# Normalising attention after the product with V: inverted sums broadcast through DRAM

## The chip, the cores and the metric

The kernel runs on one core of a Trainium2 chip. The metric is the device time of one execution in microseconds, the median of several runs. The core has TensorE (matrix products; the profile calls it PE and its weight loads PEld), VectorE (DVE), ScalarE (ACT) and GpSimd (POOL), and DMA engines that move data between DRAM and the on-chip memory. DMAs are started from the instruction queues of SyncE (SP) and ScalarE. TensorE writes only into PSUM, whose banks have to be emptied by VectorE or ScalarE before they can be used again. Each engine works its own queue strictly in order; an instruction that waits holds all behind it.

## The reference

Eight batches with eight heads each, 576 positions, head size 64. Attention is causal by blocks of 64 positions, and its output feeds a gated layer:

```python
scores = (1 / sqrt(D)) * q @ k.T            # per batch and head
scores = where(block_i >= block_j, scores, -1e9)
scores = scores - max(scores, axis=-1)
attn = exp(scores)
attn = attn / (sum(attn, axis=-1) + 1e-9)
x = (attn @ v)                              # heads side by side: 4608 x 512
out = (sigmoid(x @ w_gate) * (x @ w_val)) @ w_out   # d_ff = 1536
```

Everything is 32-bit. The division by the row sum can stand before the product with v or behind it: each row of the output is scaled by one number either way.

## The kernel before

**Attention** goes by pairs of heads, 32 pairs in all: a pair fills the 128 partitions with 2 x 64. For each pair K and Q are brought into transposed form (`prep`), and `attend` does the rest. The queries lie in blocks of 128 rows, i = 0 to 3, and a tail of 64 rows for each of the two heads (block 4, both heads in one tile, `Pt`). Block i sees 128 (i + 1) keys. `s_blocks` and `s_tail` form the scores in PSUM (L356), overwrite what is masked (L387, L389), take the negative row maximum (L367, L403, VectorE), and take the exponential on ScalarE (L370, L405), which leaves P in SBUF and, with `accum_out`, the row sums in columns of `sm`. Since `sm` has the queries on its partitions, a row's sum is a number per partition for P.

`recip` adds 1e-9 to columns of `sm` and inverts them (L409, L410, VectorE), twice a pair. `norm` multiplies the four P tiles by them per head (L419 on VectorE; in pairs 4 to 7 block 3 goes to ScalarE, L417), and `norm_t` the tail (L480 on VectorE, L478 on ScalarE). Then TensorE transposes P in pieces of 128x128 (`tr_main`, `tr_low`, `tr_tail`, L245), ScalarE copies the transposed pieces to `G1` and `G0` (`copy_out`, L345), and `av` multiplies: V is the stationary operand, G the moving one, and the result is x^T, head dimension on the partitions and queries along the row, in two pieces of 320 and 256 columns. ScalarE copies it from PSUM to `xT` (L345, called from L463); `finish` makes from it the rounded part `XH` (L470), the rest `XL` (L473, GpSimd), and stores `xT` to DRAM (L471).

**The gated layer** has 12 blocks of d_ff. Four are done in the same pass (`mlp1`, L126 and L135), batch by batch, their matmuls dealt out one by one between those of attention. The other eight follow after attention in a second pass (L838, L896), which reads x back from DRAM. Both take weights that are first converted from how they lie in the inputs (`convert`, L106 to L118; `sums_gv`, `split_gv` and others, L631 to L699), mostly on VectorE. The glue `h` (L147) empties PSUM on VectorE.

**Order.** A pair has a slot of 12 ticks. `FIRST` (pairs 0 to 6), `TURN` (pair 7) and `REST` (from pair 8) list the steps of a slot with the ticks behind each: a name in small letters is a step of this pair p; `AV` and the ones with `TR` in capitals belong to pair p - 1. So A V of a pair runs in the slot of the next one. In each tick some matmuls of `mlp1` are dealt out. Weight conversion, loads of q, k and v (two and three pairs ahead, on SyncE's queue) and, at the end, the early work for the second pass hang on these ticks. A planner orders each engine's instructions by a simulated timeline; it keeps to data dependencies, buffers that have to come free, and to explicit orders: `behind(a, b)` puts instruction a after b on its engine. `mark(engine, ins)` notes the last attention instruction of an engine in `last`, and other work is put behind it: the conversions (L78 and L106, L108), K's and Q's transposes (L276), and the early work:

```python
            if when == (0, TICKS - 2):
                sums_gv(*early[0], alone=last["DVE"])
            if when == (1, 1):
                x_sums(early_x[0], nc.vector, last["DVE"])
            if when == (1, 4):
                sums_gv(*early[1], alone=last["DVE"])
```

Here (0, t) is tick t of the last pair's slot and (1, t) is tick t of one more slot, in which only A V of the last pair is left; its ticks come after A V.

PSUM has three double banks for attention (scores, transposes and A V take them in turn) and two single banks for `mlp1`.

Of the kernel before, what the change touches and what calls it, by code (L numbers as in the profile page):

```python
# [20 lines left out]
N2 = 384  # L21
# [9 lines left out]
         ("tr3", 1))  # L31
REST = (("s", 3), ("t", 1), ("AV", 2), ("tr3", 1), ("k", 0), ("tr2", 1), ("q", 0), ("trl", 2), ("trt", 2))
TURN = (("s3", 1), ("TR2", 1), ("k", 0), ("s2", 1), ("TRt", 1), ("q", 0), ("t", 1), ("TRl", 1), ("sl", 1), ("AV", 1),
        ("tr3", 1), ("tr2", 1), ("trl", 1), ("trt", 1))
# [6 lines left out]
def attn_glu_kernel(ctx: ExitStack, tc: tile.TileContext, q, k, v, w_gate, w_val, w_out, out):  # L41
# [119 lines left out]
    with ExitStack() as s2:  # L161
# [29 lines left out]
        for QB in QBs + [x.bitcast(F32) for x in QBS]:  # L191
            nc.gpsimd.memset(QB, 0.0)
        wg, wv = {}, {}
# [137 lines left out]
        def attend(p):  # L331
# [6 lines left out]
            sm = at.tile([P, 12], F32, name="sm", bufs=2)  # L338
            keep = {}
            col = {3: 0, 2: 2, 4: 4, 1: 5, 0: 7}  # L340
            rest = p > N_FIRST
            by_act = NP <= p <= N_FIRST
# [20 lines left out]
            def softmax(ps, i, c):  # L363
                n = P * (i + 1)
                c0 = col[i]
                Pi = keep[i] = p_tile(i)
                mark("DVE", nc.vector.tensor_reduce(out=nm[:, c0:c0 + 2], in_=ps[:, :, c:c + n], axis=AX.X, op=ALU.max,  # L367
                                                    negate=True))
                for h in range(2):
                    mark("ACT", nc.scalar.activation(out=Pi[:, h], in_=ps[:, h, c:c + n], func=AF.Exp,  # L370
                                                     bias=nm[:, c0 + h:c0 + h + 1], accum_out=sm[:, c0 + h:c0 + h + 1]))
# [21 lines left out]
            def s_tail():  # L393
# [4 lines left out]
                for half in range(2):  # L398
                    for k, (x, y) in enumerate(ops):
# [6 lines left out]
                                                 func=AF.Exp, bias=nm[:, c0:c0 + 1], accum_out=sm[:, c0:c0 + 1]))  # L406

            def recip(a, n):
                nc.vector.tensor_scalar_add(sm[:, a:a + n], sm[:, a:a + n], 1e-9)  # L409
                nc.vector.reciprocal(sm[:, a:a + n], sm[:, a:a + n])  # L410

            def norm(i):
                c0 = col[i]
                Pi = keep[i]
                for h in range(2):
                    if i == 3 and by_act:
                        mark("ACT", nc.scalar.mul(out=Pi[:, h], in_=Pi[:, h], mul=sm[:, c0 + h:c0 + h + 1]))  # L417
                        continue
                    mark("DVE", nc.vector.tensor_scalar_mul(Pi[:, h], Pi[:, h], sm[:, c0 + h:c0 + h + 1]))  # L419
# [55 lines left out]
            def norm_t():  # L475
                r = sm[:, col[4]:col[4] + 1]
                if by_act:
                    nc.scalar.mul(out=keep[4], in_=keep[4], mul=r)  # L478
                else:
                    nc.vector.tensor_scalar_mul(keep[4], keep[4], r)  # L480

            def first_step(what):
                if what[0] == "s":
                    if what == "sl":
                        norm(3)
                    s_blocks({"s3": (3,), "s2": (2,), "sl": (1, 0)}[what])
                elif what == "t":
                    s_tail()
                    recip(0, 5)
                elif what == "tr3":  # L490
                    norm(2)
                    norm_t()
                    tr_main(3)
                elif what == "tr2":
                    recip(5, 4)
                    norm(1)
                    norm(0)
                    tr_main(2)
                else:
                    step(what)  # L500

            def step(what):
                if what == "s":
                    s_blocks((3,), (2,), (1, 0))
                    recip(0, 4)
                    norm(3)
                elif what == "t":
                    s_tail()
                    norm(2)
                    recip(4, 5)  # L510
                elif what == "tr3":
                    tr_main(3)
                    norm(1)
                    norm(0)
                    norm_t()
# [10 lines left out]
            return step if rest else first_step  # L526
# [13 lines left out]
        def tiles_o(i):  # L540
            if not co_:
                co_.append(at.tile([P, 5, 512], U32, name="co", bufs=1))
            co, j = co_[0], 2 * (i % 2)
            return (co[:, j:j + 2].rearrange("p a (n w) -> p (a n) w", w=2), co[:, 4], None,
# [484 lines left out]
```

## Time and profile before

| | |
|---|---|
| runs, median (lowest to highest) | 1223.63 us (1222.17 to 1224.56) |
| the profiled execution: its span, first to last instruction | 1223.3 us |
| TensorE busy | 1171.9 us, 96% |
| VectorE busy | 861.9 us, 70% |
| ScalarE busy | 651.2 us, 53% |
| GpSimd busy | 337.9 us, 28% |
| attention and the first pass | to about 656 us |
| second pass | from about 656 us |

The profile is of one execution, whose own time is known by its span alone. Times are in microseconds from its start; in groups of instructions `out<-in` names the tiles, and after the bar come the busy time, the mean in ns of one instruction, and the idle time of the engine just ahead of the group, with what ended it. "A <- B" in the lists of waits says that A waited until B was done.

### The profile page before, as it was taken

What the parts mean: (1) busy time and instruction counts of PE and PEld (TensorE: products, weight loads), DVE (VectorE), ACT (ScalarE), POOL (GpSimd) and SP (SyncE); (2) the same over time, 40 slices, a digit from 0 to 9 for tenths busy, and PEclk for the clock granted to TensorE, in tenths of its full rate; (3) what the DMA queues carried; (4) which work ended last, traced back from release to release, by engine and by line L of the source; (5) the groups of instructions that cost most, each with busy time, mean ns of one, the idle gap of its engine ahead of it and who ended that gap; (6) DMA issues with size and microseconds to landing.
All of it is one profiled execution on the core that took longest, in us unless ns stands there. A gap on an engine that the chain in (4) does not pass through costs nothing.

```text
span 1223.3 us, 20662 instructions
## 1 busy us (share of the span) xinstructions
PE 1171.9 (96%) x7421; PEld 1030.8 (84%) x7421; DVE 861.9 (70%) x1691; ACT 651.2 (53%) x1523; POOL 337.9 (28%) x409
## 2 busy tenths in 40 slices
PE   6889899999999999999999999999999999999996
PEld 4567678888888888889798899999999998998995
DVE  6888876577575875757898967857866755755742
ACT  5778766666665776756544544444444322422420
POOL 1113232223222332313401132132132152361441
PEclk8889999999999999999999999999999999999998
DMA  8543242423424333332343245145197154264243
GB/s 212 130 103 90 53 109 43 113 68 63 109 60 102 70 76 85 76 86 82 97 147 128 62 160 190 41 166 187 37 326 289 55 180 140 77 197 136 79 148 103
DMA packets 239125, 142.91 MB, mean 117 GB/s; under 512 B 183600, under 2 KB 204080, under 8 KB 238384
## 3 DMA queue, kind: packets, MB, share of 16 engines
q1 hardware_dynamic: 227968, 122.43, 35.7%
q10 hardware_dynamic: 11056, 19.17, 4.4%
q8 instruction: 59, 0.97, 0.3%
q14 instruction: 42, 0.34, 0.1%
HBM read 94.37 MB, written 47.19 MB: 116 GB/s over the span
## 4 chain that ended last, share of the span: by engine, by line
PE 74%; DVE 14%; DMA 4%; ACT 4%; issue 2%; SPq 1%; POOL 1%; POOLq 0%; DVEq 0%; ACTq 0%
PE b L838 23%; PE bank L242 11%; PE m L126 11%; PE m L896 9%; PE m L135 7%; PE b L896 5%; PE bank L245 4%; DMA pr<-part_d 2%; DVE P L419 2%; ACT P L370 2%; DVE XL L730 2%; PE bank L126 1%; DVE nm L367 1%; PE bank L135 1%; DVE KQ L274 1%
## 5 line engine op out<-in xcount | busy, mean ns | idle before, releaser
L838 PE MATMUL b<-XH,w 128*128 128x384 f32 x1344 | 349.9, 336 | 5.4 <-DVE v L874 2.7
L838 PEld LDWEIGHTS b<-XH,w 128*128 128x128 f32 x1344 | 243.7, 188 | 12.6 <-DVE v L874 6.6
L838 PE MATMUL b<-XL,w 128*128 128x384 f32 x672 | 223.7, 335 | 0.0
L370 ACT ACTIVATE P<-bank,nm 128x512 f32<-128x512 f32 (+3 forms) x256 | 132.9, 533 | 86.4 <-DVE nm L367 74.7
L838 PEld LDWEIGHTS b<-XL,w 128*128 128x128 f32 x672 | 126.1, 188 | 1.2
L896 PE MATMUL m<-wo,hH 128*128 128x512 f32 x384 | 124.9, 391 | 0.0
L345 ACT COPY G<-bank 128x768 f32<-128x768 f32 (+3 forms) x160 | 106.2, 700 | 27.4 <-PE bank L245 26.0
L367 DVE TENSOR_REDUCE nm<-bank 128x2 f32<-128x1024 f32 (+3 forms) x128 | 104.8, 819 | 8.2 <-ACT P L370 5.7
L126 PE MATMUL m<-XH,wv 128*128 128x288 f32 x448 | 104.8, 304 | 2.9 <-DVE h L147 2.9
L126 PE MATMUL m<-XH,wg 128*128 128x288 f32 x448 | 106.1, 305 | 0.6 <-ACT t L145 0.6
L153 POOL TENSOR_TENSOR hL<-h,hH 128x288 fp32r<-128x288 f32 (+1 forms) x56 | 49.0, 875 | 182.4 <-ACT hH L152 171.7
L242 PE MATMUL bank<-G,VS 128*64 128x320 f32 (+4 forms) x896 | 95.2, 364 | 0.0
L245 PE MATMUL bank<-ident,P 128*128 128x128 f32 x640 | 90.0, 280 | 4.1 <-DVE P L419 3.6
L911 POOL TENSOR_TENSOR pr<-pr,pr 128x512 f32<-128x512 f32 x36 | 48.2, 1342 | 162.7 <-DMA pr<-part_d 117.0
L419 DVE TENSOR_SCALAR P<-P,sm 128x256 f32<-128x256 f32 (+3 forms) x248 | 87.8, 414 | 1.7
L242 PEld LDWEIGHTS bank<-G,VS 128*64 128x64 f32 x896 | 56.4, 138 | 36.8 <-issue 4.1
L245 PEld LDWEIGHTS bank<-ident,P 128*128 128x128 f32 x640 | 76.7, 144 | 12.4 <-ACT wo L117 3.1
L861 ACT ACTIVATE g<-g 128x384 f32<-128x384 f32 x72 | 37.2, 524 | 87.2 <-DVE g L874 62.2
L896 PEld LDWEIGHTS m<-wo,hH 128*128 128x128 f32 x384 | 71.9, 188 | 13.8
L729 ACT CAST XH<-XB 128x1536 fp32r<-128x1536 f32 (+2 forms) x72 | 65.9, 939 | 29.3 <-DVE XB L727 22.5
L473 POOL TENSOR_TENSOR XL<-xT,XH 128x576 fp32r<-128x576 f32 x32 | 47.2, 1476 | 123.5 <-ACT XH L470 107.8
L126 PEld LDWEIGHTS m<-XH,wv 128*128 128x128 f32 x448 | 74.8, 188 | 6.2 <-DVE h L147 4.2
(176 smaller groups left out, 2543.6 us busy)
## 6 DMA issues: line engine op xcount, KB each, us to landing
pr<-part_d SPq DMA_DIRECT2D x72, 256.0 KB, 3.7
xT_d<-xT ACTq DMA_DIRECT2D x32, 288.0 KB, 2.8
XB<-xT_d SPq DMA_DIRECT2D x16, 576.0 KB, 5.5
part_d<-ost SPq DMA_DIRECT2D x36, 256.0 KB, 4.0
out_dram<-ost SPq DMA_DIRECT2D x36, 256.0 KB, 2.8
VS<-in_v_dram SPq DMA_DIRECT2D x64, 128.0 KB, 2.5
part_d<-ost ACTq DMA_DIRECT2D x32, 256.0 KB, 2.1
rqk<-in_k_dram SPq DMA_DIRECT2D x108, 72.0 KB, 2.6
```

Of the source, the lines that this page charges most:

```text
L126: mm = nc.tensor.matmul(ps, lhsT=lh, rhs=rh, start=(i == 0), stop=(i == n - 1))
L135: mm = nc.tensor.matmul(ps, lhsT=lh[:, f, t * P:(t + 1) * P], rhs=rh, start=(i == 0), stop=(i == n - 1))
L153: lower.tensor_sub(out=hL, in0=h2[:, cols], in1=hH.bitcast(F32))
L242: pe_last[:] = [nc.tensor.matmul(*args, **kw).ins]
L245: pe_last[:] = [nc.tensor.transpose(*args).ins]
L345: mark("ACT", nc.scalar.copy(out=dst, in_=src))
L367: mark("DVE", nc.vector.tensor_reduce(out=nm[:, c0:c0 + 2], in_=ps[:, :, c:c + n], axis=AX.X, op=ALU.max, negate=True))
L370: mark("ACT", nc.scalar.activation(out=Pi[:, h], in_=ps[:, h, c:c + n], func=AF.Exp, bias=nm[:, c0 + h:c0 + h + 1], accum_out=sm[:, c0 + h ...
L419: mark("DVE", nc.vector.tensor_scalar_mul(Pi[:, h], Pi[:, h], sm[:, c0 + h:c0 + h + 1]))
L729: nc.scalar.copy(out=XO[j][0][:, a:b], in_=x)
L838: mm = nc.tensor.matmul(ps, lhsT=lh, rhs=rh, start=(first and k == 0), stop=(k == n - 1), skip_group_check=not first)
L896: mm = nc.tensor.matmul(po[t], lhsT=lh[:, f, t * P:(t + 1) * P], rhs=rh, start=(half == 0 and i == 0), stop=(half == 1 and i == 5))
```

## The change

P is left undivided: `norm` and `norm_t` are gone, and so is the split of steps between `first_step` and `step`. The sums go to columns 4h + i (column 8 for the tail) of two fixed tiles of 128x32 that take turns. A new step `r`, without ticks of its own, stands in each list right after `tr3` of the same pair; it adds and inverts all nine columns at once, transposes the tile in blocks of 32x32 on VectorE, writes the nine rows to DRAM in four DMAs, and reads them back in four DMAs, each row sent to the 64 partitions of its head, so that the tile `rb` has the inverse of a query's sum in the query's column on every partition. `av` then takes x^T out of PSUM with a multiplication by `rb` on VectorE, where ScalarE had copied it; the multiplication is marked as VectorE's last, and so is the transpose.

To make room, the raw w_out pieces of the first pass are converted in two tiles that are used for x later on, and not in a tile of their own.

```diff
-        ("tr3", 1))
+        ("tr3", 1), ("r", 0))
...
-            sm = at.tile([P, 12], F32, name="sm", bufs=2)
+            sm = SMs[p % 2]
+            rb = at.tile([P, S], F32, name="rb", bufs=2)
...
-            def norm(i):
-                c0 = col[i]
-                Pi = keep[i]
-                for h in range(2):
-                    if i == 3 and by_act:
-                        mark("ACT", nc.scalar.mul(out=Pi[:, h], in_=Pi[:, h], mul=sm[:, c0 + h:c0 + h + 1]))
-                        continue
-                    mark("DVE", nc.vector.tensor_scalar_mul(Pi[:, h], Pi[:, h], sm[:, c0 + h:c0 + h + 1]))
+            def recip():
+                nc.vector.tensor_scalar_add(sm[:, :9], sm[:, :9], 1e-9)
+                nc.vector.reciprocal(sm[:, :9], sm[:, :9])
+                rT = at.tile([P, 32], F32, name="rT", bufs=2)
+                mark("DVE", nc.vector.transpose(out=rT, in_=sm))
+                r_d = dram.tile([9, P], F32, name="r_d", bufs=2)
+                for j in range(4):
+                    nc.sync.dma_start(out=r_d[:, 32 * j:32 * j + 32], in_=rT[32 * j:32 * j + 9])
+                for o, n, src in ((0, 4 * P, r_d[:8].rearrange("(h i) q -> h (i q)", h=2)),
+                                  (4 * P, D, r_d[8].rearrange("(h q) -> h q", h=2))):
+                    for h in range(2):
+                        nc.sync.dma_start(out=rb[rows(h), o:o + n], in_=src[h].partition_broadcast(D))
...
-                    copy_out(xT[:, q0:q0 + n], pv[:, i, :n])
+                    mark("DVE", nc.vector.tensor_mul(out=xT[:, q0:q0 + n], in0=pv[:, i, :n], in1=rb[:, q0:q0 + n]))
...
-            def norm_t():
-                r = sm[:, col[4]:col[4] + 1]
-                if by_act:
-                    nc.scalar.mul(out=keep[4], in_=keep[4], mul=r)
-                else:
-                    nc.vector.tensor_scalar_mul(keep[4], keep[4], r)
...
-                co_.append(at.tile([P, 5, 512], U32, name="co", bufs=1))
+                co_.extend(cv.tile([P, 6, N2], U32, name="XB", bufs=2) for _ in range(2))
```

More of the change, by code (lines that the diff above doesn't have):

```diff
@@ L30 @@
 FIRST = (("s3", 1), ("TR2", 1), ("k", 1), ("s2", 1), ("TRt", 1), ("q", 1), ("t", 1), ("TRl", 1), ("sl", 1), ("AV", 2),
-         ("tr3", 1))
-REST = (("s", 3), ("t", 1), ("AV", 2), ("tr3", 1), ("k", 0), ("tr2", 1), ("q", 0), ("trl", 2), ("trt", 2))
+         ("tr3", 1), ("r", 0))
+REST = (("s", 3), ("t", 1), ("AV", 2), ("tr3", 1), ("r", 0), ("k", 0), ("tr2", 1), ("q", 0), ("trl", 2), ("trt", 2))
 TURN = (("s3", 1), ("TR2", 1), ("k", 0), ("s2", 1), ("TRt", 1), ("q", 0), ("t", 1), ("TRl", 1), ("sl", 1), ("AV", 1),
-        ("tr3", 1), ("tr2", 1), ("trl", 1), ("trt", 1))
+        ("tr3", 1), ("r", 0), ("tr2", 1), ("trl", 1), ("trt", 1))
 N_FIRST = 7
@@ L192, in attn_glu_kernel @@
             nc.gpsimd.memset(QB, 0.0)
+        SMs = [at.tile([P, 32], F32, name=f"sm{i}") for i in range(2)]
+        for SM in SMs:
+            nc.gpsimd.memset(SM, 0.0)
         wg, wv = {}, {}
@@ L337, in attend @@
             nm = at.tile([P, 12], F32, name="nm", bufs=2)
-            sm = at.tile([P, 12], F32, name="sm", bufs=2)
+            sm = SMs[p % 2]
+            rb = at.tile([P, S], F32, name="rb", bufs=2)
             keep = {}
-            col = {3: 0, 2: 2, 4: 4, 1: 5, 0: 7}
+            col = {i: 2 * i for i in range(5)}
             rest = p > N_FIRST
-            by_act = NP <= p <= N_FIRST
             def copy_out(dst, src):
@@ L370, in softmax @@
                     mark("ACT", nc.scalar.activation(out=Pi[:, h], in_=ps[:, h, c:c + n], func=AF.Exp,
-                                                     bias=nm[:, c0 + h:c0 + h + 1], accum_out=sm[:, c0 + h:c0 + h + 1]))
+                                                     bias=nm[:, c0 + h:c0 + h + 1], accum_out=sm[:, 4 * h + i:4 * h + i + 1]))
             def s_blocks(*groups):
@@ L473, in finish, with step @@
                 nc.gpsimd.tensor_sub(out=XL[:, hp], in0=xT, in1=XH[:, hp].bitcast(F32))
-            def norm_t():
-                r = sm[:, col[4]:col[4] + 1]
-                if by_act:
-                    nc.scalar.mul(out=keep[4], in_=keep[4], mul=r)
-                else:
[L480 to L485, printed above, removed]
+            def step(what):
+                if what == "s":
+                    s_blocks((3,), (2,), (1, 0))
+                elif what[0] == "s":
                     s_blocks({"s3": (3,), "s2": (2,), "sl": (1, 0)}[what])
@@ L488, in first_step @@
                     s_tail()
[L489 to L510, printed above, removed]
+                elif what == "r":
+                    recip()
                 elif what == "tr3":
                     tr_main(3)
-                    norm(1)
-                    norm(0)
-                    norm_t()
                 elif what == "tr2":
@@ L524, in step @@
                     finish()
-            return step if rest else first_step
+            return step
         W_out = []
@@ L541, in tiles_o @@
             if not co_:
-                co_.append(at.tile([P, 5, 512], U32, name="co", bufs=1))
-            co, j = co_[0], 2 * (i % 2)
-            return (co[:, j:j + 2].rearrange("p a (n w) -> p (a n) w", w=2), co[:, 4], None,
+                co_.extend(cv.tile([P, 6, N2], U32, name="XB", bufs=2) for _ in range(2))
+            co = [x.rearrange("p a n -> p (a n)") for x in co_]
+            j = 1024 * (i % 2)
+            return (co[0][:, j:j + 1024].rearrange("p (n w) -> p n w", w=2), co[1][:, :512], None,
                     mp.tile([P, 512], F32, name="csq", tag="ost", bufs=2))
```

5 lines of the change are left out of this document (1 added, 4 removed).

## The prediction

> **What bounds the kernel now.** I read the page first, then the busy time by stretch, TensorE's waits, the chain of waits, the groups by shape and the timelines at both ends of the attention.
>
> ```profile
> span 1223.3 us, 20662 instructions
> PE 1171.9 (96%) x7421; PEld 1030.8 (84%) x7421; DVE 861.9 (70%) x1691; ACT 651.2 (53%) x1523; POOL 337.9 (28%) x409
> ```
>
> TensorE is busy for 1171.9 of 1223.3 us, and the change gives it neither more nor less to do. So a gain can only come out of its 51.4 us of idle time and out of stretches with a lower granted clock. Where these lie:
>
> ```profile
> 25.00:92.00 67.00, 56.16 (x365) 38.62 (x366) 56.16 (x124) 51.70 (x139) 12.09 (x14) 0.90 0.54 126
> 92.00:176.00 84.00, 76.95 (x543) 60.36 (x544) 68.32 (x146) 63.24 (x166) 24.47 (x32) 0.98 0.33 79
> 176.00:560.00 384.00, 382.41 (x2966) 332.35 (x2963) 259.60 (x552) 259.50 (x699) 114.24 (x188) 1.00 0.36 80
> 560.00:597.00 37.00, 33.95 (x278) 29.76 (x274) 31.11 (x67) 23.77 (x67) 10.13 (x16) 0.99 0.28 88
> 597.00:656.00 59.00, 56.95 (x339) 49.26 (x338) 53.90 (x118) 24.10 (x48) 8.62 (x4) 0.98 0.41 133
> 656.00:700.00 44.00, 41.63 (x226) 39.53 (x225) 42.76 (x75) 23.33 (x41) 6.03 (x4) 1.00 0.23 74
> ```
>
> After the stretch come TensorE, its weight loads, VectorE, ScalarE, GpSimd, then the granted clock. From 176 to 560 us, pairs 9 to 30, TensorE waits 1.6 us of 384: there the change can win nothing. From 25 to 176 us, pairs 0 to 8, it waits 10.8 + 7.1 = 17.9 us, and the clock of 0.90 and 0.98 costs 56.2 x 0.10 + 77.0 x 0.02 = 7.1 us more. From 597 to 700 us VectorE is busy for 96.7 of 103 us: work put there has hardly a gap to go to.
>
> ```profile
> PE bank L242 <- ACT P L370: 8.4, 4, 3.8
> ```
>
> And from the chain of waits (start, length, what), the first and the last of 18 pieces:
>
> ```profile
> 33.06 1.45 DVE P L419 x4
> ...
> 156.87 0.43 DVE Pt L480
> ```
>
> The first line is TensorE's largest wait between 10 and 92 us (sum, times, longest): for ScalarE's exponentials, which wait for row maxima, which stand in VectorE's queue among divisions. The 18 pieces are the divisions of P (L419 and L480, and L417 on ScalarE); they make 15.7 us of the chain.
>
>
> **The change part by part.** Durations from the groups by shape (busy time, mean ns):
>
> ```profile
> L419 DVE TENSOR_SCALAR P<-P,sm 128x256 f32<-128x256 f32 (+3 forms) x248 | 87.8, 414 | 1.7
> L480 DVE TENSOR_SCALAR Pt<-Pt,sm 128x576 f32<-128x576 f32 x28 | 30.6, 1091 | 0.0
> L417 ACT ACTIVATE P<-P,sm 128x512 f32<-128x512 f32 x8 | 5.4, 735 | 0.0
> L409 DVE TENSOR_SCALAR sm<-sm 128x5 f32<-128x5 f32 x32 | 6.7, 209 | 26.0 <-ACT Pt L405 18.8 <-ACT P L370 7.2
> L410 DVE RECIPROCAL sm<-sm 128x5 f32<-128x5 f32 x32 | 6.0, 188 | 1.0
> L274 DVE STREAM_TRANSPOSE KQ<-rqk 128x576 f32<-128x576 f32 x54 | 38.8, 750 | 0.0
> L869 DVE TENSOR_TENSOR v<-b,p 128x384 f32<-128x384 f32 x24 | 13.3, 555 | 12.8 <-PE b L838 7.1 <-ACT p L854 3.8 <-POOL hL L846 1.9
> L153 DVE TENSOR_TENSOR hL<-h,hH 128x288 fp32r<-128x288 f32 x4 | 1.8, 450 | 0.0
> L345 ACT COPY xT<-bank 128x320 f32<-128x320 f32 x32 | 13.7, 427 | 16.9 <-PE bank L242 16.6 <-issue 0.2
> L345 ACT COPY xT<-bank 128x256 f32<-128x256 f32 x32 | 12.4, 389 | 0.0
> ```
>
> Removed: 87.8 + 30.6 = 118.4 us of divisions on VectorE, 32 of 64 pairs of small additions and inversions (32 x 0.40 = 12.7 us), on ScalarE the scalings of pairs 4 to 7 and two copies per pair (13.7 + 12.4 us by means). Added on VectorE: one transpose of 128x32 per pair, which no row shows; between 0.19 (the 128x5 inversion) and 0.75 (the 128x576 transpose), I take 0.2, since its size is near the former. And two products out of PSUM with 320 and 256 columns: the 384-wide sum out of PSUM takes 0.555, a 288-wide one 0.450, so 1.1 ns a column, 0.485 + 0.415 = 0.90 us (bounds: 576 columns in proportion to the 384-wide row, 0.83, and 2 x 0.555 = 1.11). VectorE loses 131 us and gets 32 x 1.1 = 35, a net 96 us, 3 us a pair. The other moves cost nothing: the converted w_out pieces go through the two x tiles, which nothing else uses before 560 us, and GpSimd, busy for 28%, fills two 128x32 tiles more at the start. The broadcasts read 288 KB a pair, 9.4 MB in all, through DMA engines that are busy for 0.36 of the time in the long stretch.
>
> [...] The longest wait in the row above is 3.8 us, and the clock there is 0.90. [...]
>
> First stage (25 to 176 us). Between 0 (ScalarE's path, 114.9 us busy in these 151, is as long) and 15.7 us can come out of the chain; I take half, 7.8, because VectorE, at 124.5 of 151 us the fullest after TensorE, is relieved most. Waiting falls by 7.8 of 17.9, so I take the same share of the clock's 7.1, 3.1 us. Gain 10.9.
>
> The new wait: x^T's product needs the sums, by way of DRAM, when A V is done, in the next pair's slot.
>
> ```profile
> 23.35 0.21 ACT L370 ACTIVATION_READ_ACCUMULATOR P<-bank,nm 128x1 f32 x1
> 31.29 2.93 PE L242 MATMUL bank<-G,VS 128*64 128x320 f32 x28
> 53.11 0.26 ACT L370 ACTIVATION_READ_ACCUMULATOR P<-bank,nm 128x1 f32 x1
> 61.02 2.93 PE L242 MATMUL bank<-G,VS 128*64 128x320 f32 x28
> 253.50 0.23 ACT L405 ACTIVATION_READ_ACCUMULATOR Pt<-bank,nm 128x1 f32 x1
> 253.93 0.61 SPq L214 DMA_DIRECT2D VS<-in_v_dram  x1
> 268.72 2.93 PE L242 MATMUL bank<-G,VS 128*64 128x320 f32 x28
> part_d<-ost ACTq DMA_DIRECT2D x8, 128.0 KB, 2.4
> VS<-in_v_dram SPq DMA_DIRECT2D x32, 32.0 KB, 2.1
> rqk<-in_k_dram SPq DMA_DIRECT2D x5, 32.0 KB, 4.9
> ```
>
> The route: three small VectorE operations 0.6 us, four writes at most 4 x 0.61 = 2.4 on SyncE's queue, landing 2.1 (smallest row), four reads 2.4, landing 2.4 (128 KB row): 9.9 us. SyncE's queue holds loads of q, k and v for two and three pairs ahead behind it, which have a pair's time to spare. For a late pair the last sum is out at 253.73 and the next A V ends at 271.65: 17.9 us, 8 to spare, some of which SyncE's own loads take; cost 0. If that cover were gone, each further us would hold VectorE, the row maxima behind the product, and a PSUM bank, 24 times over. For pair 0 the last sum is out at 23.56 and A V ends at 34.22, 10.7 us, while loads land in 4.9 us as in the k row: 9.9 + (4.9 - 2.1) + (4.9 - 2.4) = 15.2, so 4.5 late. For pair 2 it is 53.37 to 63.95, 10.6 us, just enough. The next user of A V's PSUM bank comes only two transposes later, and the early conversions, which are ordered behind the marked product, shift with it: between 0 and 4.5, I take 2.
>
> The tail. x_sums(early_x[0]) and sums_gv(early[1]) are held behind the last VectorE instruction that was marked (`last["DVE"]`). Before, that is a division of pair 31; afterwards the marked one is x^T's product of pair 31, because A V runs ahead of both and the copy, which was ScalarE's, is now marked on VectorE.
>
> ```profile
> 590.57 0.85 PE L245 MATMUL bank<-ident,P 128*128 128x128 f32 x6 [0.74 <-DVE P L419]
> 590.96 0.42 DVE L631 TENSOR_SCALAR cT<-raw 128x512 uint32<-128x512 uint32 x1
> 595.41 0.40 PE L126 MATMUL m<-XH,wv 128*128 128x288 f32 x1 [2.00 <-DVE h L147]
> 600.78 0.48 DVE L678 TENSOR_TENSOR cT<-cT 128x128 f32<-128x128 f32 x2
> 600.91 1.31 PE L242 MATMUL bank<-G,VS 128*64 128x64 f32 x16
> 625.64 0.45 DVE L147 SCALAR_TENSOR_TENSOR h<-t,bank 128x288 f32<-128x288 f32 x1
> 626.14 0.40 PE L126 MATMUL bank<-XH,wg 128*128 128x288 f32 x1 [0.19 <-DVE h L147]
> 657.21 1.09 DVE L685 TENSOR_TENSOR w<-cT,w 128x896 fp32r<-128x896 f32 x1 [3.47 <-ACT w L684]
> ```
>
> From 590.96 to 601.2 VectorE makes two sets of weight sums and one of x (10.3 us with one h of 0.4). Of these, one set (4.2) and the x sums (three 384-wide sums, 1.4 with their overlap) go behind a product that can't start until A V ends at 602.2. VectorE then runs dry at about 590.96 - 1.5 (the last divisions) + 10.3 - 5.6 = 594.2, and after 602.2 it has 5.6 + 0.9 = 6.5 us more to do, in a stretch without gaps, before the h of 625.64, for which TensorE already waits (0.19). Against it, the 0.74 and 2.00 us that TensorE waited for VectorE's queue go, 2.7 us: net 6.5 - 2.7 = 3.8 us later. Behind it VectorE has a gap of 3.5 us (657.21), so I count no more than that. Bounds: -2.7 (the planner puts h ahead of the sums) to +6.5 (the 2.7 are not won). I take 3.8, since that row has TensorE waiting already.
>
> Sum: -10.9 + 2 + 0 + 3.8 = -5.1 us. The profiled execution spans 1223.3 us, which makes 1218.2; the three runs have their median 0.3 above that span, at 1223.63, so for a median I say **1218.5 us**.
>
> **The rivals.** *A large gain*: all 15.7 us leave the chain, the clock gives back 6, the sums for pair 0 come in time, and h is put ahead in the tail: 15.7 + 6 + 2.7 = 24.4, so 1199; this case begins half-way, at 1209. For it: VectorE is in the chain wherever TensorE waits. Against: ScalarE, with 51.7 of 67 us, stands next. *No change*: the first stage wins only 5.8, and the late sums (2) and the tail (3.8) take it back: 1223.6. For it: the 384 us with a full TensorE. *The tail decides, slower*: VectorE's queue after the last A V, 6.5 us longer without the 2.7 won, with 1 us from the first stage: 1223.6 + 6.5 - 1 = 1229. It decides once the first stage wins less than the tail loses. For it: VectorE busy for 96.7 of 103 us. Against: the planner may sort h ahead. *The sums come late*: spacings of 10.6 us get shorter as the first stage does; if each of the 8 pairs there holds VectorE for 2 us, 16 - 10.9 + 3.8 = 8.9, so 1232. Against: the route of 9.9 us has room in most pairs.
>
> **How the numbers follow.** Two runs of this kernel can be told apart from about 0.2%, 2.4 us. Forecast (1209 to 1221.2) 0.45, large gain 0.08, no change (1221.2 to 1226) 0.18, tail decides 0.20, late sums 0.09. So faster 0.53, same 0.18, slower 0.29. The forecast's own range is 1209 to 1221. The range of 8 in 10 takes in the tail's case up to 1230 and the edge of the large gain, 1208; outside are most of the large gain (0.07), most of the late sums (0.07) and a rest of the tail's (0.06).
>
> **What would show it.** Right: groups L419, L480 and L417 gone, products of near 0.9 us a pair, VectorE's total lower by about 96 us; TensorE's idle from 25 to 176 us near 10 instead of 17.9 and its clock above 0.90 in the first part; 176 to 560 us as long as before, with no wait of VectorE for the broadcast tile after pair 2; VectorE idle for some 7 us ahead of the last product, and TensorE's wait for h near 626 us grown to several us. Wrong: waits of VectorE on the broadcast in pairs 9 to 30 (the route is longer than 10 us), a first stage as long as before (ScalarE's path sets it), or no idle VectorE ahead of the last product (the order behind it doesn't bind).

## The result and the profile after

The changed kernel takes 1216.81 us (median of 6 runs, 1212.38 to 1218.58) against 1223.13 us (median of 6, 1222.11 to 1224.56) for the kernel before: a ratio of 0.9945, 95% interval 0.9931 to 0.9959, so 5 to 8 us less. The forecast was 1218.5. The size is right; what it is made of is not. The stages below are read from the rows of the two profiled executions in which pair 9 and pair 31 begin (their first score matmul) and in which the first pass ends (its last matmul starts). The timeline of TensorE before (start, length, instruction):

```profile
165.53 0.50 PE L242 MATMUL bank<-KH,QH 64*128 64x512 f32 x2
...
576.74 0.49 PE L242 MATMUL bank<-KH,QH 64*128 64x512 f32 x2
...
653.82 0.39 PE L135 MATMUL bank<-wo,hH 128*128 128x512 f32 x1
```

and after:

```profile
163.55 0.50 PE L245 MATMUL bank<-KH,QH 64*128 64x512 f32 x2
...
570.74 0.49 PE L245 MATMUL bank<-KH,QH 64*128 64x512 f32 x2
...
647.01 0.39 PE L135 MATMUL bank<-wo,hH 128*128 128x512 f32 x1
```

| stage | before | after | difference | forecast |
|---|---|---|---|---|
| start to pair 9 | 165.5 | 163.6 | -2.0 | -8.9 (-10.9 + 2) |
| pair 9 to pair 31, "the way" below | 411.2 | 407.2 | -4.0 | 0 |
| pair 31 to the end of the first pass | 77.1 | 76.3 | -0.8 | +3.8 |
| from there to the end of the span (1223.3, 1214.1) | 569.5 | 567.1 | -2.4 | 0 |

The spans differ by 9.2 us, the medians by 6.3. The first line lies within the spread that a start of pair 9 shows between profiles of the same code (below the table of experiments). The last line is not put down to the change: over the runs below that part lasts 565.0 to 569.7 us, and its lowest value (565.0) comes from a kernel with all the divisions of before.

The page of the changed kernel, busy times of the engines, and its groups by shape:

```profile
PE 1166.7 (96%) x7421; PEld 1031.1 (85%) x7421; DVE 771.9 (64%) x1447; ACT 626.8 (52%) x1447; POOL 333.7 (27%) x411
```

```profile
L468 DVE TENSOR_TENSOR xT<-bank,rb 128x320 f32<-128x320 f32 x32 | 14.9, 466 | 9.8 <-DMA rb<-r_d 5.5 <-PE bank L245 4.3
L468 DVE TENSOR_TENSOR xT<-bank,rb 128x256 f32<-128x256 f32 x32 | 13.1, 411 | 0.0
...
L417 DVE STREAM_TRANSPOSE rT<-sm 128x32 f32<-128x32 f32 x32 | 6.7, 208 | 0.8
```

The prices were right: 0.466 + 0.411 = 0.88 us for the two products (forecast 0.90), 0.21 for the transpose (0.2), and VectorE is relieved of 861.9 - 771.9 = 90.0 us (96). One product in 32 waited for its broadcast, for 5.5 us. The busy time by stretch after (columns as before: TensorE, its weight loads, VectorE, ScalarE, GpSimd, granted clock):

```profile
25.00:92.00 67.00, 52.40 (x344) 35.22 (x341) 47.88 (x91) 45.81 (x126) 9.89 (x13) 0.89 0.59 143
92.00:176.00 84.00, 79.46 (x577) 63.81 (x576) 63.55 (x123) 56.85 (x151) 23.17 (x33) 0.99 0.43 100
176.00:560.00 384.00, 383.93 (x2993) 335.28 (x2994) 194.37 (x393) 251.52 (x668) 114.20 (x190) 1.00 0.42 97
```

From 25 to 176 us TensorE now idles 14.6 + 4.5 = 19.1 us; before it was 17.9, and the forecast said 10. Its clock of 0.89 and 0.99 costs 52.4 x 0.11 + 79.5 x 0.01 = 6.6 us instead of 7.1. In the long stretch VectorE is 65 us less busy, and TensorE gets 2993 matmuls into 384 us where there were 2966.

Pair 0 is where the first stage stands still. The timeline of the changed kernel there:

```profile
25.22 0.19 DVE L417 STREAM_TRANSPOSE rT<-sm 128x32 f32<-128x32 f32 x1
...
30.22 1.91 SPq L420 DMA_DIRECT2D r_d<-rT  x4
...
35.38 2.42 SPq L424 DMA_DIRECT2D rb<-r_d  x4
...
39.83 0.82 DVE L468 TENSOR_TENSOR xT<-bank,rb 128x320 f32<-128x320 f32 x2 [5.45 <-DMA rb<-r_d]
...
40.71 1.01 PE L245 MATMUL bank<-KQ 64*128 64x384 f32 x2 [4.18 <-DVE xT L468]
...
43.45 1.21 DVE L370 TENSOR_REDUCE nm<-bank 128x2 f32<-128x1024 f32 x1
```

The inverted sums are ready at 25.4 us; the product starts at 39.83. The writes leave at 30.22 only: SyncE's queue issues loads of q and k until 30.13, and from 32.2 to 35.3 five more loads stand between the writes and the reads. TensorE waits 4.18 us for the PSUM bank. The row maxima of the next scores, whose matmuls were done at 35.3, stand behind the product in VectorE's queue and, behind that, behind three steps of a weight conversion (40.57 to 43.5); they start at 43.45. In the stretches that follow, the granted clock stands at a half for 10.2 us:

```profile
26.00:39.70 13.70, 9.83 (x76) 6.68 (x74) 4.98 (x11) 8.83 (x27) 0.47 (x2) 1.00 0.73 176
39.70:49.90 10.20, 6.57 (x21) 4.11 (x23) 8.67 (x14) 5.16 (x14) 1.47 (x1) 0.50 0.64 161
49.90:60.20 10.30, 8.42 (x64) 5.06 (x64) 7.80 (x17) 8.24 (x22) 2.48 (x3) 1.00 0.57 114
```

### The profile page after: what moved, and what is told of

Read it like the earlier page. It is cut to its first block, busy times and chain, and to the rows that moved or that the text cites. A ratio compares the mean times of both kernels' runs of the same rounds, so it can differ in the third digit from the quotient of the medians.

```text
span 1214.1 us, 20793 instructions
## 1 busy us (share of the span) xinstructions
PE 1166.7 (96%) x7421; PEld 1031.1 (85%) x7421; DVE 771.9 (64%) x1447; ACT 626.8 (52%) x1447; POOL 333.7 (27%) x411
## 4 chain that ended last, share of the span: by engine, by line
PE 76%; DVE 13%; DMA 4%; ACT 3%; issue 2%; SPq 1%; POOL 1%; POOLq 0%; DVEq 0%; ACTq 0%
PE b L814 22%; PE m L126 14%; PE bank L245 13%; PE m L872 10%; PE m L135 6%; PE bank L248 6%; PE b L872 5%; DVE XL L706 2%; DMA pr<-part_d 1%; ACT P L373 1%; DVE nm L370 1%; DMA raw<-in_moe_w_val_dram 1%; DMA XB<-xT_d 1%; POOL pr L887 1%; DVE cT L616 1%
## 5 line engine op out<-in xcount | busy, mean ns | idle before, releaser
L153 POOL TENSOR_TENSOR hL<-h,hH 128x288 fp32r<-128x288 f32 (+1 forms) x56 | 41.9, 749 | 202.1 <-ACT hH L152 191.3
L126 PEld LDWEIGHTS m<-XH,wg 128*128 128x128 f32 x448 | 75.9, 190 | 3.1 <-issue 1.6
L706 DVE TENSOR_TENSOR XL<-XB,XH 128x1536 fp32r<-128x1536 f32 (+2 forms) x72 | 77.6, 1085 | 1.1 <-ACT XH L705 0.6
```

The costliest lines, as they stand in the source:

```text
L126: mm = nc.tensor.matmul(ps, lhsT=lh, rhs=rh, start=(i == 0), stop=(i == n - 1))
L706: sub = nc.vector.tensor_sub(out=XO[j][1][:, a:b], in0=x, in1=XO[j][0][:, a:b].bitcast(F32))
```

## The experiments

Three questions stood open: what the first stage would have won and what the way through DRAM took back; where the 4 us between pair 9 and pair 31 come from, a stage that was to win nothing; and what the order at the tail costs. All twelve runs in one table, with ratios to the kernel before on the same chip (whose median was 1222.5, 1221.6 and 1222.1 us beside the three groups of four), and the stages from one profiled execution each:

| kernel | median us | ratio (95%) | pair 9 starts | the way | pair 31 to the first pass's end |
|---|---|---|---|---|---|
| before | 1223.1 | | 165.5 | 411.2 | 77.1 |
| after | 1216.8 | 0.9945 (0.9931 to 0.9959) | 163.6 | 407.2 | 76.3 |
| pair 0's transfers by ScalarE | 1217.2 | 0.9949 (0.9931 to 0.9968) | 166.9 | 407.4 | 75.7 |
| pair 0's transfers by GpSimd | 1210.9 | 0.9905 (0.9888 to 0.9923) | 160.0 | 407.1 | 74.6 |
| no transfers, a tile of ones | 1207.9 | 0.9878 (0.9861 to 0.9896) | 158.6 | 407.1 | 74.5 |
| pair 0 divides P | 1212.4 | 0.9923 (0.9904 to 0.9943) | 161.1 | 407.3 | 73.9 |
| pairs 0 to 7's transfers by GpSimd | 1213.2 | 0.9942 (0.9922 to 0.9963) | 162.8 | 407.1 | 74.9 |
| changed way in pairs 0 to 7 only | 1223.4 | 1.0017 (1.0004 to 1.0030) | 163.9 | 411.5 | 77.8 |
| changed way in pairs 8 to 31 only | 1213.0 | 0.9929 (0.9912 to 0.9946) | 162.3 | 407.1 | 74.5 |
| before, without Pt's division | 1213.1 | 0.9931 (0.9914 to 0.9948) | 164.6 | 407.4 | 74.0 |
| before, without P1's and P0's | 1219.7 | 0.9987 (0.9975 to 1.0000) | 164.9 | 407.2 | 76.7 |
| before, Pt's division first | 1219.7 | 0.9987 (0.9975 to 0.9999) | 164.6 | 411.1 | 76.4 |
| before, Pt's division on ScalarE | 1214.1 | 0.9945 (0.9928 to 0.9962) | 163.9 | 407.2 | 73.9 |
| after, last product not marked | 1217.1 | 0.9951 (0.9934 to 0.9967) | 165.0 | 407.2 | 74.9 |

A start of pair 9 has to be read with its spread: six profiles with the first stage of before in them lie between 162.3 and 165.5 (mean 164.3), three with the first stage of the change between 163.6 and 165.0 (mean 164.1). The way repeats within 0.4 us wherever the code of that stage is the same.

### Pair 0's transfers from another queue

```diff
-                    nc.sync.dma_start(out=r_d[:, 32 * j:32 * j + 32], in_=rT[32 * j:32 * j + 9])
+                    (nc.scalar if p == 0 else nc.sync).dma_start(out=r_d[:, 32 * j:32 * j + 32], in_=rT[32 * j:32 * j + 9])
```

and the same for the reads; `nc.gpsimd` in the second kernel.

> The changed kernel, with the eight transfers of pair 0 alone (the sums to DRAM and their broadcast back) issued by ScalarE instead of SyncE; 31 pairs as they are. Theory 1 (pair 0's product is late because its transfers stand behind loads in SyncE's queue): the writes are issued near 26 us instead of 30.2, the reads well ahead of 35.4, the product starts between 33.5 and 36 us instead of 39.8, and the program ends 3 to 6 us below the changed kernel's 1216.8 us (the 4.2 us that TensorE waited for the product, and part of the 10.2 us at half clock behind it). Rival 1 (the transfers themselves take the time, wherever they are issued): the product still starts at 38.5 us or later, the time within 1.5 us of 1216.8. Rival 2 (the route is not what the first stage lost; the wait moves to the next thing that is late): the product is early and pair 9's first score matmul still starts within 1 us of 163.6 us, the time within 1.5 us of 1216.8.

> As the run with ScalarE's queue, but pair 0's eight transfers are issued by GpSimd, which has next to nothing else to do before 40 us. Theory 1: the product starts between 33.5 and 37 us and the time is 3 to 6 us below 1216.8 us, unless GpSimd's issuing is dearer than SyncE's (0.35 to 0.6 us for one); then it shows in the spacing of its issues. Rival 1: product at 38.5 us or later, time within 1.5 us of 1216.8. Rival 2: product early, time within 1.5 us of 1216.8.

The timeline of the kernel in which GpSimd issues them, and, under it, the time from issue to landing of its four writes (smallest, median, largest):

```profile
25.13 0.19 DVE L417 STREAM_TRANSPOSE rT<-sm 128x32 f32<-128x32 f32 x1
...
25.92 2.30 POOL L420 DMA_DIRECT2D r_d<-rT  x4
...
34.03 1.56 POOL L424 DMA_DIRECT2D rb<-r_d  x3 [1.41 <-DMA r_d<-rT]
...
35.50 1.23 DVE L370 TENSOR_REDUCE nm<-bank 128x2 f32<-128x1024 f32 x1
...
40.38 0.82 DVE L468 TENSOR_TENSOR xT<-bank,rb 128x320 f32<-128x320 f32 x2 [3.65 <-DMA rb<-r_d]
...
41.25 1.33 PE L248 MATMUL bank<-ident,Pt 128*128 128x128 f32 x5 [3.44 <-DVE xT L468]
```

```profile
DMA to landing us min/median/max: 4.8/5.5/6.1
```

Theory 1 fell on the point that it named. The writes left 4.3 us earlier than from SyncE and the product started no earlier, at 40.38 instead of 39.83, because each transfer took about 5 us to land and the reads had to wait for that. From ScalarE the first write left at 28.13, the last reads from 35.45 on, and the product came at 39.36. Here the issuing itself cost: ScalarE stood idle for 4.06 us, a wait that ended with the writes, and TensorE waited 5.26 us for its exponentials:

```profile
30.02 0.62 ACT L117 CAST wv<-cgv 128x512 fp32r<-128x512 f32 x1 [4.06 <-DMA r_d<-rT]
...
32.53 1.65 PE L245 MATMUL bank<-KQ 64*128 64x256 f32 x8 [5.26 <-ACT P L373]
```

So the route took 14 to 15 us from the inverted sums in all three, but not by the same parts: from the first write to the product it was 9.6 us on SyncE, behind 4.8 us of queue, 11.2 on ScalarE and 14.5 on GpSimd. GpSimd's transfers also run as another kind (the list of DMA queues has 288 packets of `software_dynamic`, which the changed kernel doesn't have), and when SyncE's landed isn't on record. Whether SyncE's own transfers would be faster if they stood ahead of its loads was not tried, and stays a rival to "the transfers themselves take the time". In the run in which GpSimd issues the transfers of pairs 0 to 7, the median of the writes' landings is 1.7 us and the largest 6.2:

```profile
DMA to landing us min/median/max: 1.6/1.7/6.2
```

GpSimd's run was faster than the changed kernel all the same: 0.9905 against 0.9945, about 5 us, with intervals that don't meet. ScalarE's, at 0.9949, was not. The timeline shows by what: there the widest row maximum (1.23 us, 128x1024) stands ahead of the product in VectorE's queue, at 35.50, and in the changed kernel behind it, at 43.45. So ScalarE's exponentials ran during the wait. Summed over TensorE's waits from 25 to 62 us, that is 7.0 us instead of 10.1, and the half clock behind the wait lasts 6.8 us instead of 10.2 (1.7 us of work more, half of the 3.4): together 4.8, and pair 9 starts 3.5 earlier. The tail is 1.7 shorter too, within the spread that it has between profiles of this code (73.9 to 76.3). The edit doesn't name that order; the planner found it when the transfers stood in another queue, and no run changes the order alone.

### No way through DRAM at all

```diff
+        RB = at.tile([P, S], F32, name="rb")
+        nc.gpsimd.memset(RB, 1.0)
...
-            rb = at.tile([P, S], F32, name="rb", bufs=2)
+            rb = RB
...
-                rT = at.tile([P, 32], F32, name="rT", bufs=2)
-                mark("DVE", nc.vector.transpose(out=rT, in_=sm))
-                r_d = dram.tile([9, P], F32, name="r_d", bufs=2)
```

and without the eight transfers of each pair.

> The changed kernel without the way of the sums: the transposition and all 256 transfers are left out and x^T is multiplied by a tile of ones, so the division is left out of what is computed; the sums, their reciprocals and the products are as they were. Theory 1: no product waits, pair 0's starts between 33 and 35 us instead of 39.8, the first stage is 3 to 7 us shorter, the steady stage (pairs 9 to 30) within 0.8 us of the changed kernel's, the time 1210 to 1214 us. Rival A (the route costs nothing in the end): the time within 1.5 us of 1216.8. Rival B (the 256 transfers also cost in the steady stage, by SyncE's queue or the DMA engines): the steady stage 2 us or more shorter as well, the time below 1210 us.

In its timeline pair 0's product follows A V directly:

```profile
32.52 0.82 DVE L461 TENSOR_TENSOR xT<-bank,rb 128x320 f32<-128x320 f32 x2
```

Pair 9 starts at 158.6, the way is that of the changed kernel to 0.1 us. So without the route the first stage gains 164.3 - 158.6 = 5.7 us over the mean of the old ones, and the route takes 163.6 - 158.6 = 4.9 us back (5.5 from the mean of 164.1). Neither rival holds: the route does cost, and in the steady stage its 22 pairs of transfers cost nothing that can be seen. The time, 1207.9, is 2 us below what theory 1 allowed; the tail and second pass were shorter here too, and that I don't assign.

### Pair 0 as before, and the first eight pairs by GpSimd

The first kernel keeps both forms and takes the changed one where a flag says so; the second has the condition `p <= N_FIRST` in the edit shown above.

```diff
+            new = p > 0
+            sm = SMs[p % 2] if new else at.tile([P, 12], F32, name="so", bufs=2)
...
+                    if not new:
+                        copy_out(xT[:, q0:q0 + n], pv[:, i, :n])
+                        continue
```

> The changed kernel, but pair 0 divides P as before the change, so that no product waits for transfers at the crowded start; 31 pairs have the changed way. Theory 1b (moving the issue did not bring pair 0's product forward, so the way through DRAM itself, at this crowded moment, costs the first stage what the run without the way showed, 4.9 us to pair 9's start): pair 9 starts 2 to 5.5 us earlier than with the change (163.6 us), since pair 0's divisions take back 0 to 3 us, and the time is 1209 to 1213 us. Rival A (the divisions of pair 0 stand on the chain of waits and cost as much as the way): pair 9 within 1 us of 163.6 us, time within 1.5 us of 1216.8. Rival B (pair 1's product is the next to wait for its transfers): its wait for rb appears, 2 us or more, and pair 9 is less than 2 us earlier.

> The changed kernel with the sums' transfers of pairs 0 to 7 issued by GpSimd (pair 0's alone gave 1210.9 us). If SyncE's queue is what the other seven pairs' transfers load, the first stage ends 0.5 to 2 us earlier than with pair 0's alone (pair 9 at 160.0 us) and the time is 1208 to 1211 us; if only pair 0 matters, the time is within 1.5 us of 1210.9; if GpSimd's issuing (0.5 us each) delays its own copies for the query tile, pair 9 starts 1 us or more later than 160 us.

With pair 0 divided as before, no product waits for a broadcast, pair 1's neither; pair 9 starts at 161.1, 2.5 us earlier, and the median is 1212.4. That is theory 1b, at its lower end. Giving GpSimd the transfers of eight pairs is the third case: pair 9 at 162.8, and among TensorE's waits from 25 to 165 us stands one that the other runs don't have, for GpSimd's subtraction of x^T:

```profile
PE bank L245 <- POOL XL L478: 1.9, 1, 1.9
```

The good order is there in this run as well: the widest row maximum stands at 34.40, ahead of the product at 40.16. What it loses comes later, with the wait above and with pair 8's slot, which takes 23.7 us instead of 22.0.

### Each stage's part of the change alone

The same flag, `new = p <= N_FIRST` and `new = p > N_FIRST`.

> Pairs 0 to 7 have the changed way, pairs 8 to 31 divide P as before the change. Theory 1c (the first stage's part of the change is worth nothing in sum: pair 0's way through DRAM takes back what the divisions give): pair 9 starts at 163 to 166 us, the way to pair 31's start is 410.5 to 412 us as before the change, and the time within 3 us of the kernel before. Rival (the first stage gains what the forecast said, 8.9 us): pair 9 at 159 us or earlier, the time 6 us or more below the kernel before.

> Pairs 0 to 7 divide P as before the change, pairs 8 to 31 have the changed way. Theory 1 (the gain of the profiled runs splits by stage: first stage -2.0 us, steady stage -4.0, tail and second pass the rest): pair 9's first score matmul starts at 165.5 us (+-1) as before the change, the way from there to pair 31's is 407.2 us (+-0.7) instead of 411.2, the time 1216 to 1219.5 us. Rival (the steady stage only inherits what the first stage left, so its gain goes with the first stage's): the way is 410 us or more and the time within 1.5 us of the kernel before.

The halves multiply to the whole: 1.0017 x 0.9929 = 0.9946. The first stage's half is worth nothing, a little less than nothing (+2 us, 0.5 to 3.7). All of the change's gain comes from pairs 8 to 31, where the forecast had put zero up to pair 30 and a loss of 3.8 us behind it, and the way shows the same 407.1 us there without the first stage's help. Its median, 1213.0, is lower than theory 1 said, and so is pair 9's start, 162.3 where 165.5 was expected: the same code's spread, read off one profile.

### What the steady stage gains by

Between pair 9 and pair 31 the kernel before loses its 4 us in five slots, those of pairs 14, 19, 22, 27 and 30, each 0.73 to 0.85 us longer than after the change (pair 14: 280.55 - 263.03 = 17.52 us, after 16.78). Its timeline in the first of them, all on VectorE and GpSimd but the last row:

```profile
273.15 1.01 DVE L419 TENSOR_SCALAR P<-P,sm 128x256 f32<-128x256 f32 x4
...
274.06 1.42 POOL L473 TENSOR_TENSOR XL<-xT,XH 128x576 fp32r<-128x576 f32 x1 [4.61 <-ACT XH L470]
...
274.08 1.72 DVE L480 TENSOR_SCALAR Pt<-Pt,sm 128x576 f32<-128x576 f32 x1
...
275.72 1.42 DVE L274 STREAM_TRANSPOSE KQ<-rqk 128x576 f32<-128x576 f32 x2
...
277.07 0.41 DVE L147 SCALAR_TENSOR_TENSOR h<-t,m 128x288 f32<-128x288 f32 x1
...
277.53 0.40 PE L126 MATMUL m<-XH,wv 128*128 128x288 f32 x1 [0.31 <-DVE h L147]
```

Pt's division starts 0.02 us after GpSimd's subtraction and ends 0.32 us after it, in 1.72 us; then come two transposes, then the h that TensorE waits for. Of the 0.74 us that the slot loses, 0.31 shows as idle time. Four kernels tell apart what of this counts. Each is the kernel before with one edit for pairs 8 to 31. Pt's division left out, in the step `tr3`:

```diff
 tr_main(3)
 norm(1)
 norm(0)
-norm_t()
```

P1's and P0's left out:

```diff
 tr_main(3)
-norm(1)
-norm(0)
 norm_t()
```

Pt's division first:

```diff
 tr_main(3)
+norm_t()
 norm(1)
 norm(0)
-norm_t()
```

And in `norm_t`, Pt's division given to ScalarE:

```diff
-                if by_act:
+                if by_act or rest:
```

> The kernel before, without the division of the last query rows' P (Pt, 128x576) in pairs 8 to 31; this leaves that division out of what is computed. Theory 2 (the steady stage lost its 4 us where this one division, 1.23 us on average there, stands beside GpSimd's subtraction for the low half of x^T and is stretched, up to 1.72 us, ahead of h): the way from pair 9's start to pair 31's falls from 411.2 us to 407.0 to 408.5. Rival (every division counts alike, and the 4 us came from all 4.2 us of divisions of a pair): a fall of about a quarter to a third of 4.0 us, to 409.8 or more. Rival 2 (the gain came from ScalarE, relieved of the copies of x^T): no fall, 410.7 us or more.

> The kernel before, without the divisions of P1 and P0 in pairs 8 to 31 (four instructions, 2 x 350 + 2 x 280 ns = 1.26 us of VectorE for a pair, as much as Pt's 1.23); this leaves those divisions out of what is computed. Theory 2 (it is Pt's division beside GpSimd): the way from pair 9's start to pair 31's stays at 410.2 us or more. Rival (every division counts alike): about a quarter to a third of the 4.0 us, to 409.8 to 410.3 us. If it falls as far as without Pt's division, VectorE's queue there needs only some 1.2 us less, wherever they come from.

> The kernel before, whole, with one thing changed: in pairs 8 to 31 the division of Pt stands ahead of those of P1 and P0 in VectorE's queue instead of behind them, so the same work is done in another order and Pt's division starts about 1 us earlier. Theory 2a (what costs is the stretch of Pt's division beside GpSimd's subtraction, ahead of h): its mean in the steady stage falls from 1.23 us to 0.8 or less, and the way from pair 9's start to pair 31's from 411.2 us to 407.0 to 409. Theory 2b (it is the amount of division that stands ahead of h, 1.2 us less is needed): the way stays at 410.2 us or more. Third case: the stretch passes to the divisions of P1 and P0, which then run beside GpSimd (more than 0.45 us on average for the 256 wide ones, now 0.35), and the way stays at 410.2 us or more as well.

> The kernel before, whole, with Pt's division in pairs 8 to 31 given to ScalarE, which does it already in pairs 4 to 7; nothing else of the change. Theory 2 (all that the steady stage gains, it gains by this one division leaving VectorE): the way from pair 9's start to pair 31's is 407.0 to 408 us instead of 411.2, and the time 1212 to 1218 us, no worse than the whole change's 1216.8. Rival (ScalarE, 259.5 us busy of the 384 from 176 us on, then makes the exponentials or the copies late): 409.5 us or more, and a new wait of TensorE for ScalarE of 0.5 us or more in a pair.

The groups by shape from 176 to 560 us of the kernel before:

```profile
L480 DVE TENSOR_SCALAR Pt<-Pt,sm 128x576 f32<-128x576 f32 x21 | 25.8, 1227 | 0.0
...
L419 DVE TENSOR_SCALAR P<-P,sm 128x128 f32<-128x128 f32 x42 | 10.0, 280 | 0.0
```

of the kernel with Pt's division first:

```profile
L419 DVE TENSOR_SCALAR P<-P,sm 128x128 f32<-128x128 f32 x42 | 25.4, 641 | 0.0
...
L480 DVE TENSOR_SCALAR Pt<-Pt,sm 128x576 f32<-128x576 f32 x20 | 10.4, 520 | 0.7
```

and of the one without P1's and P0's:

```profile
L480 DVE TENSOR_SCALAR Pt<-Pt,sm 128x576 f32<-128x576 f32 x21 | 11.4, 542 | 0.7
```

Turning the order round moves the stretch on and saves nothing: Pt's division falls from 1.227 to 0.520 us, and the two of P0 grow by 2 x (0.641 - 0.280) = 0.72 us, as much as Pt's lost. The timeline shows them end behind GpSimd's subtraction again, and h no better off:

```profile
272.26 0.52 DVE L480 TENSOR_SCALAR Pt<-Pt,sm 128x576 f32<-128x576 f32 x1
...
272.69 2.17 DVE L419 TENSOR_SCALAR P<-P,sm 128x256 f32<-128x256 f32 x4
...
273.17 1.41 POOL L473 TENSOR_TENSOR XL<-xT,XH 128x576 fp32r<-128x576 f32 x1 [4.61 <-ACT XH L470]
...
274.78 1.42 DVE L274 STREAM_TRANSPOSE KQ<-rqk 128x576 f32<-128x576 f32 x2
...
276.60 0.40 PE L126 MATMUL m<-XH,wv 128*128 128x288 f32 x1 [0.27 <-DVE h L147]
```

That is the third case of its expectation, and the way stays at 411.1. In both timelines the divisions that meet the subtraction end behind it: Pt's at 275.80 against 275.48 in the kernel before, the last of P0's at 274.86 against 274.58 here. From 176 to 560 us of the kernel before, 13 of Pt's 21 divisions start inside the subtraction, take 1.36 to 1.73 us and end 0.31 to 0.32 us behind it; the other 8 take 0.51. The product that the change put in their place stands ahead of the subtraction, which reads its result (39.83 and 41.51 us for pair 0), and lasts 405 to 495 ns in all 64 instances: no row here shows a stretched product.

Taking either amount away wins the whole 4 us: without Pt's division the way is 407.4, without P1's and P0's it is 407.2. So "every division alike" (a quarter to a third) falls, and what the last sentence of that expectation allowed holds: 1.2 us a pair less is enough, and it need not be Pt's division that is left out. The second kernel doesn't disprove the meeting with GpSimd, though. Its planner put h ahead of Pt's division, which there starts 0.25 us before the subtraction and isn't stretched:

```profile
273.62 0.44 DVE L147 SCALAR_TENSOR_TENSOR h<-t,m 128x288 f32<-128x288 f32 x1
...
274.56 0.52 DVE L480 TENSOR_SCALAR Pt<-Pt,sm 128x576 f32<-128x576 f32 x1
```

What goes with the gain is where this h starts, counted from the start of pair 14: 14.04 us in the kernel before and 14.01 with Pt's division first, where the slot is slow; 12.40 without Pt's division, 11.25 without P1's and P0's, 11.53 after the change. Without the stretch alone h would start at 14.04 - (1.72 - 0.52) = 12.84, an estimate from these rows, and the slot loses only 0.74. So removing the meeting might do with all divisions left; that wasn't tried.

For the time it does matter which is left out. With Pt's division off VectorE the median falls by 8 us or more, with P1's and P0's off it by 2. The difference lies behind pair 31: 74.0 us to the first pass's end against 76.7, and 566.5 against 569.4 from there on, which these runs don't explain. In the four kernels that keep Pt's division on VectorE in these pairs that part lasts 76.4 to 77.8 us; in the others, the changed kernel's 76.3 aside, 73.9 to 75.7.

Given to ScalarE, Pt's division needs nothing left out: h starts at 12.40 again, and the way is 407.2 us, the time 1214.1, ratio 0.9945, the same as the whole change. ScalarE bore it without a new wait; TensorE is as full there as after the change, with 50 us more of VectorE's work:

```profile
176.00:560.00 384.00, 383.84 (x2993) 335.46 (x2991) 244.02 (x535) 273.28 (x728) 115.52 (x189) 1.00 0.37 82
```

### The tail

```diff
-                    mark("DVE", nc.vector.tensor_mul(out=xT[:, q0:q0 + n], in0=pv[:, i, :n], in1=rb[:, q0:q0 + n]))
+                    mul = nc.vector.tensor_mul(out=xT[:, q0:q0 + n], in0=pv[:, i, :n], in1=rb[:, q0:q0 + n])
+                    if p < len(pairs) - 1:
+                        mark("DVE", mul)
```

> The changed kernel, with the product of the last pair (31) left out of the list of marked instructions, so that the sums of the last stage's first operands are not held behind it. The prediction's step (6.5 us of VectorE's work held behind that product makes the tail later): TensorE's waits for h at 588.9 (1.68 us) and 625.6 (1.28 us) shrink, and from pair 31's first score matmul to the end of the first pass the kernel is 1 to 3 us shorter. Rival (the planner already puts what is urgent first, the hold costs nothing): within 0.8 us of the changed kernel's tail and of its 1216.8 us. Third case (the product itself now comes late behind the sums): the tail 1 us or more longer.

The changed kernel's timeline shows the hold, and what the planner made of it:

```profile
588.94 0.41 PE L126 MATMUL m<-XH,wv 128*128 128x288 f32 x1 [1.68 <-DVE h L147]
...
594.46 0.83 DVE L468 TENSOR_TENSOR xT<-bank,rb 128x320 f32<-128x320 f32 x2 [3.22 <-PE bank L245]
...
616.02 0.45 DVE L147 SCALAR_TENSOR_TENSOR h<-t,bank 128x288 f32<-128x288 f32 x1
...
617.97 5.16 DVE L706 TENSOR_TENSOR XL<-XB,XH 128x1536 fp32r<-128x1536 f32 x4
...
625.55 0.40 PE L126 MATMUL bank<-XH,wg 128*128 128x288 f32 x1 [1.28 <-DVE h L147]
```

VectorE runs dry for 3.22 us and the held sums follow the product, but the h's of 613.6 and 616.0 come ahead of the long differences of 617.97 (in the kernel before, one h stands in the 14 us ahead of them, at 615.1), and TensorE waits 1.28 us near 626 instead of 0.19. That wait belongs to the hold: it is 1.1 to 1.6 us in all seven profiles with the changed tail and the hold, and gone in the run without it. But there TensorE's other wait for h, 1.68 us, grew to 2.46 instead. The tail of that run, 74.9, is 1.4 us shorter than the changed kernel's, which would be the first case of the expectation; yet the other six profiles with the hold have 73.9 to 75.7, so the 1.4 us are not shown to come from it. The time, 1217.1, can't be told from the changed kernel's.

### The fastest version

The changed kernel with pair 0's transfers issued by GpSimd, 1210.9 us, ratio 0.9905 (0.9888 to 0.9923), beats both kernels. Its gain over the change goes with an order that the planner happened to find, and the run with eight pairs shows how easily it is lost elsewhere (0.9942). It can't be told apart from the kernel in which pair 0 divides P as before (0.9923, 0.9904 to 0.9943).

## Why the prediction came out right, and where it was wrong

- **First stage, -10.9: mis-sized.** "I take half, 7.8" of the 15.7 us of divisions on the chain, and 3.1 of clock. Without the way through DRAM the stage gains 5.7 in all, divisions and clock together, about half of the sum.
- **Sums of pair 0, "between 0 and 4.5, I take 2": mis-sized.** The route's total came out (15.2 us worked out from the last sum, from 23.4 to 39.8, 16.4, measured; 4.5 us late worked out, 5.45 waited), but by other parts, which is luck: the sum put SyncE's loads behind the transfers and at nothing, and they stood ahead of the writes for 4.8 us and of the reads for 3.3. The cost was 4.9, by one profile of the run without transfers, above the range's end: the late product also held the row maxima behind it in VectorE's queue and was followed by 10.2 us at half clock. The sentence on what a further us would hold had named the maxima, and was used for the pairs after 9 but not for pair 0. Together these two terms were -8.9; the change applied to these pairs alone shows +2 us in the runs.
- **Clock.** 6.6 us lost instead of 7.1: the 3.1 forecast did not come. It had been taken as the clock's share of the waiting, and the waiting did not fall (19.1 us where there were 17.9). Nor does the half clock go with the length of the last wait in these traces. A new wait of 4.18 us came with half clock around it, but half clock also stood at the end of a wait of 2.29 us (from 60.1 to 63.5) and behind one of 1.98 (from 90.9 to 94.3), and the clock was full behind one of 2.64 us that ended at 75.0. The run without transfers has no wait over 2.4 us from 25 to 62 us and still stands at half clock for 3.4 us there (0.51 from 53.1 to 56.5).
- **Steady stage, 0: wrong, and where the gain came from.** "TensorE waits 1.6 us of 384: there the change can win nothing" took the idle share for the whole of what waits cost. The way fell by 4.0. A stall of 0.74 us shows as 0.31 us idle (the ends of matmuls are modelled in the profile): from pair 14's transposes of Pt to the next matmul 1.01 us pass before (276.52 to 277.53) and 0.46 after (275.84 to 276.30). The count in the same 384 us does show such stalls, 2966 matmuls in 382.41 us busy (128.9 ns each) against 2993 in 383.93 (128.3), and 27 matmuls at 128.3 ns are 3.5 us. No wait for the broadcast appeared in these pairs, as forecast.
- **Tail, +3.8: wrong sign.** The mechanism was there (VectorE dry ahead of the last product, 3.2 us where 7 were said; the wait near 626 grown by 1.1 where several were said), but the planner put h's first. It isn't the bound that had been named for that, -2.7: of those waits for VectorE 0.5 us went (0.74 and 2.00 became 0.59 and 1.68). What the sum lacked is the division of Pt: left out of pairs 8 to 31 of the kernel before, it takes the part behind pair 31's start from 77.1 to 74.0 us. The measured tail is 0.8 shorter.
- **Sum.** -5.1 forecast, -6.3 measured: errors of 6.9, -4.0 and -4.6 us on three stages, and a second pass that varies by some 4 us, came near to cancelling out. That the sum hit the time is luck: what holds of it are the prices of the moved operations and the zero for late sums in the steady stage. Of the rivals, a large gain and the two slower ones did not occur; the late sums of the last rival were confined to pair 0.

## What to carry to other kernels

Count work done in a stretch, not only idle time: a stage that looks 99.6% busy can still hold a per cent of stalls, and the number of matmuls in equal windows of two kernels shows it. Before moving a whole computation, try the one instruction that stands in the way: here one 128x576 division a pair, moved to ScalarE in pairs 8 to 31, gave as much as the change. A value that takes a round trip through DRAM should not be needed first where the loads are thickest (pair 0's product waited 5.45 us for it after the change, no other did), and what stands behind it in a strict queue is part of its price (the row maxima of 43.45, whose matmuls were done at 35.3).

## What was not expected of the hardware

- A division of 0.52 us took 1.72 beside GpSimd's 1.42 us subtraction, and in another order the same delay fell on other divisions (0.280 to 0.641 us): in these rows it goes with the meeting, not with the instruction.
- A transfer of 1.1 KB from GpSimd's queue landed in 1.7 us in the median and in 4.8 to 6.1 us at the crowded start, and issuing it there 4 us earlier than from SyncE brought the result no earlier.
- The granted clock stood at a half for 10.2 us around and after one wait of 4.18 us, but also for 3.4 us behind one of 1.28 us (which ended at 56.74 us in the kernel before), while it stood at full behind one of 2.64 us (75.01 in the changed kernel).
